# Expert units of 512 rows in a routed two-layer kernel: one early, seven more, then 256 and 128

## The chip, the cores and the metric

The kernel runs on one core of a Trainium2 chip. The metric is the device time of one execution in microseconds (us). Three executions of the kernel before took 748.33, 751.46 and 752.22 us; the median is 751.46 us.

## The reference

Eight batches of eight heads (576 positions, 64 values a head) go through two attentions whose results are added, and the 4608 rows of 512 values then go through one of eight experts each:

```
out_d = softmax(q_d k_d^T / 8) v_d          # q_d, k_d, v_d: means over 4 positions
out_local = softmax(masked q k^T / 8) v     # mask: |i - j| < 4
x = (repeat(out_d, 4) + out_local)          # as 4608 rows of 512
logits = x @ w_gate + modality_bias[modality_id]
e = argmax(logits);  gate = softmax(logits)[e]
out[row] = gate[row] * (relu(x[row] @ w1[e]) @ w2[e])     # w1: 8 x 512 x 1024, w2: 8 x 1024 x 512
```

Computed in numpy on the drawn inputs, the routing sends 1389 rows to expert 1, 2290 to expert 6 and 929 to expert 7, and none to the others. Of the first 2816 rows, 861, 1373 and 582 go there.

## The kernel before

**Attention and routing.** 32 head pairs pass through a software pipeline whose calls are sorted by hand-written phases (PHASE: a step's time in units of one head pair). Row batches are written to a DRAM table `xs`, and each row's number and gate are scattered (L599, one scatter for each 128 rows, from POOL) into `tab`, a DRAM list of rows by expert.

**Units.** An expert works on units of 256 rows that all belong to it. For a unit, POOL reads row numbers from `tab` (`entries`, L804, tile `tg`, one indirect DMA for each 128 rows), gathers the rows from `xs` (`gather`, L814, tile `xg`), and TensorE transposes them (`xsplit`, L836, tile `xt`). Every fp32 operand is split into a rounded fp32r part and a remainder (xh and xl, whi and wlo, hh and hl), and a product is three matmuls. Layer 1 (`compute`, L858) has the weights stationary and the rows moving: 4 chunks of 2 blocks of 4 x 3 matmuls, 96 in all, each of 256 columns. ScalarE and VectorE evict it as hh and hl (L860, L861). Layer 2 (`second`, L905) has 128 rows of the hidden layer stationary and the weights moving: 8 x 3 matmuls of 512 columns for each 128 rows. ScalarE applies the gate (L908), and POOL scatters the rows to the output (L909).

**Weights.** Each unit loads its expert's 4 MB in eight chunks of 512 KB (L763, L766 on the SP queue), each split by ScalarE (L785) and VectorE (L791). Chunks are asked for eight ahead, by `step()`, into a ring of 13.

**Order.** Two early units are taken from the first 2816 rows while the last head pairs run; their rows are gathered before `free`, the point where the attention's loading tiles are given up. Unit 0's rows are split before `free`, unit 1's after it. When the last batch is routed, one table (`late`: lists of full and half units, 25 entries over 16 columns) gives all that remains: 16 units of 256 rows and one of 128. The order is two early units, 15 units, the one of 128, and a last one of 256; a loop at the end takes what is left, and here it takes nothing (37 gathers are 18 x 2 + 1).

```
order = [(True, i, 2) for i in range(KEARLY)] + [(False, i, 2) for i in range(NFULL)]
order.insert(-1, (False, NFULL, 1))
...
            gather(i + 2)
            (moe.compute if H == 2 else moe.compute_half)(Ts[i], Ws[i], Xs[i], step, lambda: split(i + 1))
```

Of the kernel before, what the change touches and what calls it, by code (L numbers as in the profile page):

```python
# [24 lines left out]
NB = 6  # L25
# [9 lines left out]
UNIT = 256  # L35
KEARLY = 2
EB = 5
EARLY = 128 * (9 * (EB // 2) + 4 * (EB % 2))
NFULL = 18 - KEARLY
NLOOP = 8  # L40
# [4 lines left out]
SP0 = ()  # L45
HOLD = 14
NHOLD = 20
GO = 1

# [26 lines left out]
class Consts:  # L76
# [59 lines left out]
    def routing(s, tc, pool, work, psum):  # L136
# [31 lines left out]
        ip = work.tile([128, 2], I32, name="ip")  # L168
        nc.gpsimd.iota(ip, pattern=[[128, 2]], base=0, channel_multiplier=1)
        s.pos = pool.tile([128, 2], F32, name="pos")  # L170
        nc.vector.tensor_copy(s.pos, ip)

    def biases(s, tc, pool, work, rows, psum):
# [4 lines left out]
        mp = psum.tile([128, 36], F32, name="mp", tag="T", bufs=3)  # L178
# [13 lines left out]
class Attention:  # L192
# [61 lines left out]
    def vp(s, n, i):  # L254

        b, hp = divmod(n, 4)
        vw = s.vw[b % 2].rearrange("p (h k) d -> p k h d", k=NB)
        p = s.t["vp", n // 2] = s.ps.tile([96, 2, 4, D], F32, name="vp", tag="T", bufs=3)
# [9 lines left out]
    def tp(s, n, nm):  # L268

        src = s.QK[n // 2]["qk".index(nm)]  # L270
        p = s.t["tp", nm, n] = s.ps.tile([128, 512], F32, name="tp", tag="T", bufs=3)
# [10 lines left out]
    def tpt(s, n, i):  # L282

        p = s.t["tp", "t", n] = s.ps.tile([128, 2, 64], F32, name="tpt", tag="T", bufs=3)
# [42 lines left out]
    def mk(s, n, a):  # L327
        p = s.t["sc", n, a] = s.ps.tile([128, NB, WIN], F32, name="sc", tag="S", bufs=3)
        s.nc.tensor.matmul(p, s.C.identb, s.C.mask, start=True, stop=False, skip_group_check=True)
# [28 lines left out]
    def scd(s, n, i):  # L358

        qd, kd = s.t.pop(("qd", n)), s.t.pop(("kd", n))  # L360
        p = s.t["scd", n] = s.ps.tile([128, 3, 144], F32, name="scd", tag="S", bufs=3)
# [48 lines left out]
    def pdt(s, n, kc):  # L410

        p = s.t["pdt", n, kc] = s.ps.tile([96, 512], F32, name="pdt", tag="T", bufs=3)
# [47 lines left out]
class Router:  # L460
# [6 lines left out]
    def start(s, work):  # L467
# [9 lines left out]
        nc.sync.dma_start(tab.rearrange("(p o x) w -> p o x w", p=128, o=NE),  # L477
                          ft.unsqueeze(1).broadcast_to([128, NE, 36, 2]))
# [20 lines left out]
    def lgt(s, b, i):  # L499
        g0, g1 = ((0, 2), (2, s.t["G", b]))[i]  # L500
        p = s.t["lgt", b, i] = s.ps.tile([128, g1 - g0, 128], F32, name="lgt", tag="T", bufs=3)
# [75 lines left out]
    def xr(s, b, t):  # L577
        if t < s.t["G", b]:
            p = s.t["xr", b, t] = s.ps.tile([128, DM], F32, name="xr", tag="T", bufs=3)
# [36 lines left out]
    def units_of(s, c, add, n, nm):  # L616
# [4 lines left out]
        s.nc.vector.tensor_scalar(ni, ni, 8, None, op0=ALU.logical_shift_right)  # L621
# [4 lines left out]
    def table(s, n, base, U, nm, pool, tag):  # L626
# [4 lines left out]
        m = tp.tile([128, N, N], F32, name=nm + "m")  # L631
# [10 lines left out]
        nc.vector.scalar_tensor_tensor(off, excl, -float(UNIT), base, op0=ALU.mult, op1=ALU.add)  # L642
# [20 lines left out]
        nc.vector.scalar_tensor_tensor(r[:, 0], C.uf[:, :U], float(UNIT), r[:, 0], op0=ALU.mult, op1=ALU.add)  # L663
# [3 lines left out]
    def index(s, r, U, nm, count=None):  # L667

        nc, C, tp = s.nc, s.C, s.tp
        sh = [128, U, 2]  # L670
        idx = tp.tile(sh, I32, name=nm + "idx")
        nc.vector.tensor_tensor(idx, C.pos.unsqueeze(1).broadcast_to(sh), r[:, 0, :U].unsqueeze(2).broadcast_to(sh),
# [10 lines left out]
    def early(s, K):  # L683

        nc, tp = s.nc, s.tp
        n = tp.tile([128, NE], F32, name="en")
        yield from s.units_of((yield from s.counts("e")), 0, n, "e")
        r, _, excl = yield from s.table(n, s.C.ecap, K, "e", None, None)
        s.found = yield from s.index(r, K, "e")
        d = s.d = tp.tile([128, NE], F32, name="dd")  # L690
# [5 lines left out]
        yield  # L696

    def late(s, c, pool):

        nc, tp = s.nc, s.tp  # L700
        n = tp.tile([128, 2 * NE], F32, name="mn")
        base = tp.tile([128, 2 * NE], F32, name="mbase")
        whole(s.units_of(c, UNIT // 2 - 1, n[:, :NE], "m"))
        whole(s.units_of(c, UNIT - 1, n[:, NE:], "mh"))
        nc.vector.tensor_tensor(n[:, NE:], n[:, NE:], n[:, :NE], op=ALU.subtract)
        for i, x in enumerate((s.d, n[:, :NE])):
            nc.vector.scalar_tensor_tensor(base[:, NE * i : NE * i + NE], x, float(UNIT), s.C.ecap, op0=ALU.mult,  # L707
                                           op1=ALU.add)
        nc.vector.tensor_tensor(n[:, :NE], n[:, :NE], s.d, op=ALU.subtract)
# [20 lines left out]
class Moe:  # L730
    def __init__(s, tc, ctx, C, psum, xs, tab, w1, w2, out):
# [7 lines left out]
        s.xb = None  # L739
        s.nw = 13  # L740
# [55 lines left out]
    def entries(s, idx, u, H=2, T=None, h0=0):  # L796

        nc = s.nc
        T = T or s.xa.tile([128, 2, 2], I32, name="tg", bufs=4)
# [19 lines left out]
    def alt(s, key):  # L819

        n = s.turn[key] = s.turn.get(key, -1) + 1
        return s.we if n % 2 else s.xa

    def hidden(s):
        n = s.turn["h"] = s.turn.get("h", -1) + 1
        return [(s.we, s.xb)[n % 2].tile([128, 8, 256], F32R, name=nm) for nm in ("hh", "hl")]

    def xsplit(s, R, H=2):
        nc, C = s.nc, s.C
        pool = s.alt("s")  # L830
        xh = pool.tile([128, 4, 256], F32R, name="xh")
        xl = pool.tile([128, 4, 256], F32R, name="xl")
        for h in range(H):
            p = s.ps.tile([128, 4, 128], F32, name="xt", tag="T", bufs=3)
            for k in range(4):
                nc.tensor.transpose(p[:, k, :], R[:, h, 128 * k : 128 * k + 128], C.ident)  # L836
            yield
# [7 lines left out]
    def compute(s, T, W, X, step=None, mid=None):  # L845
        nc = s.nc
        xh, xl = X
        hh, hl = s.hidden()
        for c in range(4):
# [10 lines left out]
            nc.scalar.activation(hh[:, 2 * c : 2 * c + 2, :], p, AF.Relu)  # L860
            nc.vector.scalar_tensor_tensor(hl[:, 2 * c : 2 * c + 2, :], p, 0.0,  # L861
                                           hh[:, 2 * c : 2 * c + 2, :].bitcast(F32), op0=ALU.max, op1=ALU.subtract)
        if mid:
            mid()
        s.second(T, W, hh, hl, 2, step)

    def compute_half(s, T, W, X, step, mid):
# [4 lines left out]
        for g in range(2):  # L872
            r = s.xp.tile([128, 512], F32, name="o", bufs=3)
            p = s.ps.tile([128, 2, 256], F32, name="l1", tag="S", bufs=3)
# [8 lines left out]
            p = s.ps.tile([128, 4, 128], F32, name="ht", tag="T", bufs=3)  # L883
# [5 lines left out]
        mid()  # L889
        s.second(T, W, hh, hl, 1, step)  # L890

    def second(s, T, W, hh, hl, H, step):

        nc = s.nc
        for h in range(H):
            hs = slice(128 * h, 128 * h + 128)

            first = s.turn["h"] == 0
            p = s.ps.tile([128, DM], F32, name="l2", tag="S" if first else "A", bufs=3 if first else 2)
# [18 lines left out]
def build(tc, q, k, v, mid, w_gate, bias, w1, w2, out):  # L918
    nc = tc.nc
    with ExitStack() as ctx:  # L920
# [5 lines left out]
        tab = dp.tile([NSLOT, 2], I32, name="tab")  # L926
        C = Consts(tc, cp, ps)
        moe = Moe(tc, ctx, C, ps, xs, tab, w1, w2, out)
        with ExitStack() as actx:
# [71 lines left out]
            def rows(u, h):  # L1001
                R[u] = moe.gather(T[u], EARLY, h + 1, R.get(u), h)
                if h:
# [12 lines left out]
            def split(u):  # L1016
                piece(("x", u), lambda: moe.xsplit(E[u][2]), E[u].append)
# [6 lines left out]

            going = {}
# [5 lines left out]
            for i in range(26):  # L1031
# [3 lines left out]
            for i in range(2 * KEARLY):  # L1035
                call(t + 0.5 + 0.6 * i, entries, i // 2, i % 2)
                call(t + 3 + 0.6 * i, rows, i // 2, i % 2)
            for j in range(7):
                call(t + 5.8 + 0.15 * j, split, 0)
# [17 lines left out]
            for j in range(7):  # L1057
                call(free + 1.5 + 0.1 * j, split, 1)
# [23 lines left out]
            early = [E[0] + [W], E[1]]  # L1082

        order = [(True, i, 2) for i in range(KEARLY)] + [(False, i, 2) for i in range(NFULL)]
        order.insert(-1, (False, NFULL, 1))
        Es, Ts, Rs, Xs = {}, {}, {}, {}

        def gather(i):
            if i < len(order):
                ahead, u, H = order[i]  # L1090
                if ahead:
                    Es[i], Ts[i], Rs[i] = early[i][:3]
                else:
                    Es[i], Ts[i] = moe.expert(tei, u), moe.entries(tidx, u, H)
                    Rs[i] = moe.gather(Ts[i], H=H)

        def split(i):
            if i < len(order):
                Xs[i] = early[i][3] if i < KEARLY else whole(moe.xsplit(Rs[i], order[i][2]))

        def step():

            pace.append(0)
            for _ in range(SP0[len(pace) - 1] if len(pace) <= len(SP0) else 1):
                if not todo:
                    return
# [3 lines left out]
        pace = []  # L1110
        Ws = {i: [] for i in range(len(order))}
        Ws[0] = early[0][4]
        todo = [(i, c) for i in range(len(order)) for c in range(8)][len(Ws[0]) :]
        gather(0)
        gather(1)
        split(0)
        for c in range(LEAD - len(Ws[0])):
            i, c = todo.pop(0)
            Ws[i].append(moe.chunk(Es[i], c // 4, c % 4))
        for i, (_, _, H) in enumerate(order):  # L1120
            if i == 0:
                with tc.high_priority():
                    tidx, tei = ro.late(cnt, moe.xp)
            gather(i + 2)
            (moe.compute if H == 2 else moe.compute_half)(Ts[i], Ws[i], Xs[i], step, lambda: split(i + 1))
# [45 lines left out]
```

## Time and profile before

| | |
|---|---|
| median of three runs | 751.46 us |
| the profiled execution: its time | 754.67 us |
| its span, first to last instruction | 753.0 us |
| mean granted TensorE clock | 0.957 |
| TensorE matmuls busy | 705.5 us, 94% of the span |
| VectorE, ScalarE, GpSimd busy | 450.4, 429.3, 293.1 us |
| moved by DMA | 141.55 MB |

Times in the views count from the first instruction of the span. Matmuls are pipelined: the time that one occupies the engine is read from start to start, not from the length printed beside it.

### The profile page before, as it was taken

What the parts mean: (1) busy time and instruction counts of PE and PEld (TensorE: products, weight loads), DVE (VectorE), ACT (ScalarE), POOL (GpSimd) and SP (SyncE); (2) the same over time, 40 slices, a digit from 0 to 9 for tenths busy, and PEclk for the clock granted to TensorE, in tenths of its full rate; (3) what the DMA queues carried; (4) which work ended last, traced back from release to release, by engine and by line L of the source; (5) the groups of instructions that cost most, each with busy time, mean ns of one, the idle gap of its engine ahead of it and who ended that gap; (6) DMA issues with size and microseconds to landing.
All of it is one profiled execution on the core that took longest, in us unless ns stands there. A gap on an engine that the chain in (4) does not pass through costs nothing. (4 is left out here: it accounts for less than half of the span.)

```text
span 753.0 us, 21037 instructions
## 1 busy us (share of the span) xinstructions
PE 705.5 (94%) x8435; PEld 602.7 (80%) x8435; DVE 450.4 (60%) x908; ACT 429.3 (57%) x908; POOL 293.1 (39%) x385
## 2 busy tenths in 40 slices
PE   5999899999969999976999999999999999999995
PEld 3777677776747778875999889998899988999894
DVE  3677476676766695665765555655556556565520
ACT  2667587686756686536665554655545555555520
POOL 7545566637465953035533322322323233121101
PEclk8799899999998999988999999999999999999998
DMA  9899978969874544639997667776677666676500
GB/s 188 170 180 200 145 161 168 170 140 170 150 149 118 110 159 99 188 117 323 304 306 235 212 219 238 226 241 213 210 231 237 239 198 229 200 255 223 167 13 18
DMA packets 201445, 141.55 MB, mean 188 GB/s; under 512 B 133661, under 2 KB 172609, under 8 KB 201346
## 3 DMA queue, kind: packets, MB, share of 16 engines
q1 hardware_dynamic: 193090, 120.96, 62.1%
q0 software_dynamic: 8256, 19.22, 7.4%
q8 instruction: 67, 1.10, 0.7%
q14 instruction: 32, 0.26, 0.1%
HBM read 120.95 MB, written 19.47 MB: 186 GB/s over the span
## 5 line engine op out<-in xcount | busy, mean ns | idle before, releaser
L791 DVE TENSOR_TENSOR wlo<-raw,whi 128x1024 fp32r<-128x1024 f32 x130 | 158.4, 1231 | 134.3 <-ACT whi L785 133.5
L785 ACT CAST whi<-raw 128x1024 fp32r<-128x1024 f32 x130 | 135.0, 1049 | 129.0 <-PE l L858 60.9
L858 PE MATMUL l<-xh,whi 128*128 128x256 f32 x488 | 139.7, 288 | 4.3 <-DVE mn L623 3.7
L858 PE MATMUL l<-xl,whi 128*128 128x256 f32 x488 | 140.7, 289 | 0.0
L858 PE MATMUL l<-xh,wlo 128*128 128x256 f32 x488 | 140.4, 288 | 0.0
L909 POOL DMA_INDIRECT out_dram<-o,tg x37 | 40.0, 1081 | 174.4 <-ACT o L908 134.3
L858 PEld LDWEIGHTS l<-xh,whi 128*128 128x128 f32 x488 | 95.0, 195 | 5.8 <-issue 4.1
L905 PE MATMUL l<-whi,hl 128*128 128x512 f32 x256 | 99.5, 390 | 0.0
L905 PE MATMUL l<-wlo,hh 128*128 128x512 f32 x256 | 99.4, 391 | 0.0
L905 PE MATMUL l<-whi,hh 128*128 128x512 f32 x256 | 97.6, 395 | 0.0
L858 PEld LDWEIGHTS l<-xl,whi 128*128 128x128 f32 x488 | 94.9, 194 | 0.8
L858 PEld LDWEIGHTS l<-xh,wlo 128*128 128x128 f32 x488 | 95.0, 195 | 0.2 <-issue 0.2
L861 DVE SCALAR_TENSOR_TENSOR hl<-l,hh 128x512 fp32r<-128x512 f32 x72 | 49.4, 686 | 28.9 <-ACT hh L860 28.9
L804 POOL DMA_INDIRECT tg<-tab,midx x33 | 37.8, 1145 | 72.8 <-DMA out_dram<-o,tg 66.7
L860 ACT ACTIVATE hh<-l 128x512 fp32r<-128x512 f32 x72 | 42.7, 593 | 35.7 <-PE l L858 35.7
L392 POOL TENSOR_TENSOR le<-le,zr 128x384 f32<-128x384 f32 x32 | 26.7, 834 | 91.5 <-DVE zr L388 72.9
L814 POOL DMA_INDIRECT xg<-xs,tg x37 | 40.8, 1102 | 53.0 <-DMA tg<-tab,midx 35.2
L599 POOL DMA_INDIRECT tab<-ig,si x36 | 38.2, 1060 | 54.1 <-DVE mbase L707 33.7
L905 PEld LDWEIGHTS l<-wlo,hh 128*128 128x128 f32 x256 | 48.0, 188 | 10.2
L408 ACT COPY Pw<-lt 32x288 f32<-32x288 f32 x128 | 54.9, 429 | 2.2
L905 PEld LDWEIGHTS l<-whi,hh 128*128 128x128 f32 x256 | 48.1, 188 | 9.9 <-issue 0.5
L905 PEld LDWEIGHTS l<-whi,hl 128*128 128x128 f32 x256 | 48.1, 188 | 9.6
(216 smaller groups left out, 1373.5 us busy)
## 6 DMA issues: line engine op xcount, KB each, us to landing
raw<-in_moe_w_dram SPq DMA_DIRECT2D x152, 512.0 KB
vw<-in_v_dram SPq DMA_DIRECT2D x53, 192.0 KB
xs<-R SPq DMA_DIRECT2D x36, 256.0 KB
qt<-in_q_dram SPq DMA_DIRECT2D x30, 288.0 KB
kt<-in_k_dram SPq DMA_DIRECT2D x30, 288.0 KB
vw<-in_v_dram SPq DMA_DIRECT2D x15, 96.0 KB
xg<-xs,tg POOLq DMA_INDIRECT x37, 5.2
out_dram<-o,tg POOLq DMA_INDIRECT x37, 3.5
```

What stands on the lines that cost most here:

```text
L392: s.nc.gpsimd.tensor_tensor(e, e, z[:, : 2 * NB].unsqueeze(2).broadcast_to([128, 2 * NB, WIN]), op=ALU.mult)
L408: s.nc.scalar.copy(s.Pw[n % NPW][r, :, j, :SUB], s.t["lt", n][r, :, :SUB])
L599: i = nc.gpsimd.indirect_dma_start(out=s.tab[:, :], out_offset=bass.IndirectOffsetOnAxis(ap=C.si[:, t : t + 1], axis=0), in_=C.ig[:, t, :] ...
L785: nc.scalar.copy(hi, raw)
L791: nc.vector.tensor_tensor(lo, raw, hi.bitcast(F32), op=ALU.subtract)
L804: nc.gpsimd.indirect_dma_start(out=T[:, h, :], out_offset=None, in_=s.tab[:, :], in_offset=bass.IndirectOffsetOnAxis(ap=idx[:, u, h : h + ...
L814: s.gathered = nc.gpsimd.indirect_dma_start(out=R[:, h, :], out_offset=None, in_=s.xs[:n, :], in_offset=bass.IndirectOffsetOnAxis(ap=T[:, ...
L858: nc.tensor.matmul(p[:, f, :], a[:, k, fs], x[:, k, :], start=(k == 0 and i == 0), stop=(k == 3 and i == 2))
L860: nc.scalar.activation(hh[:, 2 * c : 2 * c + 2, :], p, AF.Relu)
L861: nc.vector.scalar_tensor_tensor(hl[:, 2 * c : 2 * c + 2, :], p, 0.0, hh[:, 2 * c : 2 * c + 2, :].bitcast(F32), op0=ALU.max, op1=ALU.subtract)
L905: nc.tensor.matmul(p, a[:, f, hs], x[:, f % 2, :], start=(f == 0 and i == 0), stop=(f == 7 and i == 2))
L909: nc.gpsimd.indirect_dma_start(out=s.out[:, :], out_offset=bass.IndirectOffsetOnAxis(ap=T[:, h, 0:1], axis=0), in_=o, in_offset=None, boun ...
```

## The change

The unit becomes 512 rows. One early unit (KEARLY = 1) is taken from the first 2816 rows, seven more ("pairs", NPAIR) come from a small table of their own (7 entries over 8 columns), made first; a second table (`late`, 21 entries over 16 columns) gives two units of 256, one of 128, and up to 18 for the loop. On the drawn counts the pairs are one of expert 1, four of expert 6 and two of expert 7; then one unit of 256 each of experts 1 and 6 and the one of 128 of expert 1 are left, and nothing for the loop.

Layer 1 of a 512 unit has 96 matmuls of 512 columns; layer 2 goes over four blocks of 128 rows. hh and hl have one buffer instead of two, xh and xl too. The next unit's rows are split in three places of layer 2 (two blocks, one, one) instead of one. The early unit's split stands wholly after `free`. The weight ring has 12 chunks. Table entries past the end point behind `tab`, which is 4608 rows longer, and gathers pass over rows out of bounds; the early unit's tile of rows is therefore cleared first, on POOL.

```diff
-UNIT = 256
-KEARLY = 2
+KEARLY = 1
-NFULL = 18 - KEARLY
-NLOOP = 8
+NPAIR = 8 - KEARLY
+NFULL = 2
+NLOOP = 18
-HOLD = 14
-NHOLD = 20
+HOLD = 9
+NHOLD = 16
+SPLIT = {4: (2, 1, 1), 2: (2,), 1: (2,)}
...
+    def pairs(s, c, pool):
+        nc, tp = s.nc, s.tp
+        n = tp.tile([128, NE], F32, name="pn")
+        base = tp.tile([128, NE], F32, name="pbase")
+        whole(s.units_of(c, 127, n, "p", 9))
+        nc.vector.tensor_tensor(n, n, s.d, op=ALU.subtract)
+        nc.vector.scalar_tensor_tensor(base, s.d, 512.0, s.C.ecap, op0=ALU.mult, op1=ALU.add)
+        r, _, s.pexcl = whole(s.table(n, base, NPAIR, "p", pool, "o", 512))
+        s.pn = n
+        return whole(s.index(r, NPAIR, "p", H=4))
...
-        s.nw = 13
+        s.nw = 12
...
-        R = R or s.xa.tile([128, 2, DM], F32, name="xg", bufs=2)
+        R = R or s.unit_rows()
...
-                in_offset=bass.IndirectOffsetOnAxis(ap=T[:, h, 0:1], axis=0))
+                in_offset=bass.IndirectOffsetOnAxis(ap=T[:, h, 0:1], axis=0), bounds_check=n - 1, oob_is_err=False)
...
     def hidden(s):
-        n = s.turn["h"] = s.turn.get("h", -1) + 1
-        return [(s.we, s.xb)[n % 2].tile([128, 8, 256], F32R, name=nm) for nm in ("hh", "hl")]
+        s.turn["h"] = s.turn.get("h", -1) + 1
+        return [s.xb.tile([128, 8, 512], F32R, name=nm) for nm in ("hh", "hl")]
...
+        N = 128 * H
         for c in range(4):
...
-            p = s.ps.tile([128, 2, 256], F32, name="l1", tag="S", bufs=3)
             for f in range(2):
+                if H == 4 or f == 0:
+                    p = s.ps.tile([128, 4 // H, N], F32, name="l1", tag="S", bufs=SB)
                 fs = slice(128 * f, 128 * f + 128)
                 for k in range(4):
                     for i, (a, x) in enumerate(((wh, xh), (wh, xl), (wl, xh))):
-                        nc.tensor.matmul(p[:, f, :], a[:, k, fs], x[:, k, :], start=(k == 0 and i == 0),
+                        nc.tensor.matmul(p[:, 0 if H == 4 else f, :], a[:, k, fs], x[:, k, :N], start=(k == 0 and i == 0),
                                          stop=(k == 3 and i == 2))
...
+            def clear(u):
+                R[u] = moe.unit_rows()
+                nc.gpsimd.memset(R[u], 0.0)
+            for u in range(KEARLY):
+                call(4.3 + u, clear, u)
...
-            for j in range(7):
-                call(t + 5.8 + 0.15 * j, split, 0)
...
-            for j in range(7):
-                call(free + 1.5 + 0.1 * j, split, 1)
+            for j in range(13):
+                call(free + 0.4 + 0.15 * j, split, 0)
...
+        order = [("e", i, 4) for i in range(KEARLY)] + [("p", i, 4) for i in range(NPAIR)]
+        order += [("m", i, 2) for i in range(NFULL)]
+        order.insert(-1, ("m", NFULL, 1))
...
-        gather(0)
-        gather(1)
-        split(0)
...
             if i == 0:
                 with tc.high_priority():
-                    tidx, tei = ro.late(cnt, moe.xp)
+                    lists["p"] = ro.pairs(cnt, moe.xp)
+                gather(1)
+            if i == 1:
+                lists["m"] = ro.late(cnt, moe.xp)
             gather(i + 2)
```

## Rows read from the trace of the kernel before

**Rows 1.** The page: TensorE's busy share, and its granted clock in 40 slices.
```profile
PE 705.5 (94%) x8435; PEld 602.7 (80%) x8435; DVE 450.4 (60%) x908; ACT 429.3 (57%) x908; POOL 293.1 (39%) x385
...
PEclk8799899999998999988999999999999999999998
```

**Rows 2.** Windows: start:end, length, each engine's busy us, clock, DMA share, GB/s.
```profile
321.00:332.00 11.00, 7.33 (x36) 6.83 (x34) 9.26 (x32) 4.63 (x7) 5.53 (x5) 0.69 0.29 105
332.00:355.00 23.00, 17.23 (x97) 14.50 (x95) 11.31 (x19) 10.14 (x13) 10.34 (x11) 0.91 0.80 256
...
381.05:684.14 303.09, 303.09 (x1977) 278.23 (x1976) 174.02 (x184) 162.80 (x210) 85.28 (x77) 1.00 0.69 228
```

**Rows 3.** TensorE in order of time, one settled unit: start, length, instruction, idle before.
```profile
381.05 0.28 PE L858 MATMUL l<-xh,whl 128*128 128x256 f32 x1
...
392.56 1.04 PE L836 MATMUL xt<-ident,xg 128*128 128x128 f32 x8
393.36 0.48 PE L905 MATMUL l<-whi,hh 128*128 128x512 f32 x1
...
404.36 0.28 PE L858 MATMUL l<-xh,whi 128*128 128x256 f32 x1
```

**Rows 4.** TensorE in order of time, from the early units on.
```profile
282.49 0.50 PE L858 MATMUL l<-xh,whi 128*128 128x256 f32 x2
...
298.04 0.60 PE L836 MATMUL xt<-ident,xg 128*128 128x128 f32 x4
...
308.02 1.28 PE L490 MATMUL lg<-X,wg 128*32 128x320 f32 x16
...
324.89 0.55 PE L858 MATMUL l<-xh,whi 128*128 128x256 f32 x1 [3.67 <-DVE mn L623]
...
345.70 0.39 PE L905 MATMUL l<-whi,hl 128*128 128x512 f32 x1
...
346.61 0.39 PE L905 MATMUL l<-wlo,hh 128*128 128x512 f32 x1
351.19 1.11 PE L836 MATMUL xt<-ident,xg 128*128 128x128 f32 x4 [4.19 <-DMA xg<-xs,tg]
353.38 1.12 PE L836 MATMUL xt<-ident,xg 128*128 128x128 f32 x4 [1.08 <-DMA xg<-xs,tg]
355.17 1.01 PE L858 MATMUL l<-xh,whi 128*128 128x256 f32 x3 [0.67 <-ACT xh L839]
...
684.14 0.28 PE L858 MATMUL l<-xh,whl 128*128 128x256 f32 x1
```

**Rows 5.** POOL in order of time, where the routing ends.
```profile
331.23 0.96 POOL L599 DMA_INDIRECT tab<-ig,si  x1 [0.30 <-issue]
...
338.27 0.99 POOL L909 DMA_INDIRECT out_dram<-o,tg  x1 [4.61 <-issue]
339.57 0.98 POOL L804 DMA_INDIRECT tg<-tab,midx  x1 [0.30 <-DMA raw<-in_moe_w_dram]
...
346.48 0.95 POOL L814 DMA_INDIRECT xg<-xs,tg  x1 [4.66 <-DMA tg<-tab,midx]
```

**Rows 6.** VectorE in order of time, the table of the remaining units.
```profile
321.46 0.16 DVE L612 COPY mc<-cp 128x8 f32<-128x8 f32 x1
...
327.53 0.17 DVE L638 TENSOR_TENSOR mexcl<-mincl,mn 128x16 f32<-128x16 f32 x1
327.62 0.57 DVE L651 TENSOR_TENSOR o<-mincl,uf 128x400 f32<-128x400 f32 x1
...
333.42 0.23 DVE L676 CAST mei<-mr 128x17 int32<-128x17 f32 x1
```

**Rows 7.** The page's costliest groups: the evictions of layer 1.
```profile
L861 DVE SCALAR_TENSOR_TENSOR hl<-l,hh 128x512 fp32r<-128x512 f32 x72 | 49.4, 686 | 28.9 <-ACT hh L860 28.9
...
L860 ACT ACTIVATE hh<-l 128x512 fp32r<-128x512 f32 x72 | 42.7, 593 | 35.7 <-PE l L858 35.7
```

**Rows 8.** POOL in order of time: three memsets.
```profile
5.76 3.11 POOL L218 MEMSET Pw<- 128x1152 f32 x3
```

More of the change, by code (lines that the diff above doesn't have):

```diff
@@ L614, in counts, with units_of @@
         return c
[L616 removed]
+    def units_of(s, c, add, n, nm, bits=8):
         ni = s.tp.tile([128, NE], I32, name=nm + "ni")
@@ L624, in units_of, with table @@
         yield
-    def table(s, n, base, U, nm, pool, tag):
+    def table(s, n, base, U, nm, pool, tag, unit=256):
         nc, C, tp = s.nc, s.C, s.tp
         N = n.shape[1]
-        m = tp.tile([128, N, N], F32, name=nm + "m")
+        m = (pool.tile([128, DM], F32, name=tag, bufs=3)[:, : N * N].rearrange("p (a b) -> p a b", a=N) if tag else
+             tp.tile([128, N, N], F32, name=nm + "m"))
         incl = tp.tile([128, N], F32, name=nm + "incl")
@@ L641, in table @@
         off = tp.tile([128, N], F32, name=nm + "off")
-        nc.vector.scalar_tensor_tensor(off, excl, -float(UNIT), base, op0=ALU.mult, op1=ALU.add)
+        nc.vector.scalar_tensor_tensor(off, excl, -float(unit), base, op0=ALU.mult, op1=ALU.add)
         yield
@@ L681, in index, with taken @@
         return idx, ei
[L683 to L690, printed above, removed]
+    def taken(s, n, excl, K, nm):
+        nc = s.nc
+        d = s.tp.tile([128, NE], F32, name=nm + "d")
         nc.vector.tensor_scalar(d, excl, -1.0, float(K), op0=ALU.mult, op1=ALU.add)
@@ L925, in build @@
         xs = dp.tile([NTOK + 1, DM], F32, name="xs")
-        tab = dp.tile([NSLOT, 2], I32, name="tab")
+        tab = dp.tile([NSLOT + CAP, 2], I32, name="tab")
         C = Consts(tc, cp, ps)
@@ L1030, in build @@
             t = 4 * (EB - 1) + max(P[x] for x in P if x[:2] == "st") + 0.02
-            for i in range(26):
+            for i in range(29):
                 call(min(t, 4 * (EB - 1) + P["ch2"] + 0.1) + 0.07 * i, first)
@@ L1034, in build @@
                 call(t + 1 + 0.1 * u, expert, u)
-            for i in range(2 * KEARLY):
-                call(t + 0.5 + 0.6 * i, entries, i // 2, i % 2)
-                call(t + 3 + 0.6 * i, rows, i // 2, i % 2)
-            for j in range(7):
-                call(t + 5.8 + 0.15 * j, split, 0)
+            for i in range(4 * KEARLY):
+                call(t + 0.5 + 0.6 * i, entries, i // 4, i % 4)
+                call(t + 3 + 0.6 * i, rows, i // 4, i % 4)
             for c in range(2):
@@ L1081, in build @@
                 ro.store(b, i)
[L1082 to L1086, printed above, removed]
+            early = [E[0] + [W]]
+        order = [("e", i, 4) for i in range(KEARLY)] + [("p", i, 4) for i in range(NPAIR)]
+        order += [("m", i, 2) for i in range(NFULL)]
+        order.insert(-1, ("m", NFULL, 1))
+        lists, Es, Ts, Rs, Xs, parts = {}, {}, {}, {}, {}, {}
@@ L1088, in gather @@
         def gather(i):
             if i < len(order):
[L1090 to L1097, printed above, removed]
-            if i < len(order):
-                Xs[i] = early[i][3] if i < KEARLY else whole(moe.xsplit(Rs[i], order[i][2]))
+                nm, u, H = order[i]
@@ new lines, in gather, with split @@
+                idx, ei = lists[nm]
+                Es[i], Ts[i] = moe.expert(ei, u), moe.entries(idx, u, H)
+                Rs[i] = moe.gather(Ts[i], H=H)
+        def split(i, h):
+            if i < len(order):
+                if not h:
+                    parts[i] = moe.xsplit(Rs[i], order[i][2])
+                n = len(SPLIT[order[i - 1][2]]) - 1
+                for _ in range(SPLIT[order[i - 1][2]][min(h, n)] if h <= n else 0):
+                    for x in (next(parts[i], None) for _ in range(3)):
+                        Xs[i] = x or Xs.get(i)
+                if h == order[i - 1][2] - 1:
+                    next(parts[i], None)
@@ L1101, in step @@
         def step():
[L1103 to L1106, printed above, removed]
+            if todo:
                 i, c = todo.pop(0)
                 Ws[i].append(moe.chunk(Es[i], c // 4, c % 4))
-        pace = []
         Ws = {i: [] for i in range(len(order))}
-        Ws[0] = early[0][4]
+        Es[0], Ts[0], Rs[0], Xs[0], Ws[0] = early[0]
         todo = [(i, c) for i in range(len(order)) for c in range(8)][len(Ws[0]) :]
-        gather(0)
```

123 lines of the change are left out of this document (69 added, 54 removed).

## The prediction

> **What bounds the kernel now.** The page comes first: TensorE is busy 94% of the span at a clock near full speed, and no other engine passes 60% [rows 1]. The page's chain of what ended last holds only the last few us, so I cut the span into windows. From 381.05 to 684.14 TensorE is busy every one of 303.09 us at clock 1.00, while VectorE and ScalarE are busy 174.02 and 162.80 us and DMA 0.69 [rows 2]. There the bound is TensorE's own stream, and neither fewer weight loads nor fewer splits can shorten it.
>
> In that stream I read starts [rows 3]. Layer 1 runs from 381.05 to 392.56: 11.51 us for 96 matmuls of 256 columns, 0.120 us each. Eight transposes take 0.80. Layer 2 runs from 393.36 to 404.36: 11.00 us for 48 matmuls of 512 columns, 0.229 each. Twice the columns cost 1.91 times as much, so a part of each matmul's time does not grow with its columns. A unit takes 23.31 us, and thirteen of them fill the 303.09.
>
> Ahead of it is the head, 282.49 to 355.17, where the two early units mix with the attention's end [rows 4]. TensorE waits there: 3.67 us before 324.89, 4.19 before 351.19, then 1.08 and 0.67, in all 9.6. Of these, 5.3 are waits for gathered rows. The clock is 0.69 in 321 to 332 and 0.91 in 332 to 355 [rows 2]; the first full unit after 355.17 takes 25.88 us, up to 381.05, 2.57 above the settled 23.31.
>
> So the span is 355.17 + 25.88 + 13 x 23.31 + 68.86, where 68.86 is what follows 684.14: a unit of 256, the one of 128, the last of 256, and the end. I call the start of the first unit after the early rows S; here it is 355.17.
>
> **The change part by part.** From S on, 14 units of 256 become seven of 512, and the last three units and the end stay.
>
> *Layer 1, wider.* Two units had 192 matmuls of 0.120: 23.02 us. One unit of 512 has 96 of 512 columns. Layer 2 already issues matmuls of that width, in fp32r, at 0.229 on average [rows 3]; undisturbed, four of them take 0.91 us from 345.70 to 346.61, 0.2275 each [rows 4]. That gives 21.8 to 22.0, a saving of 1.0 to 1.2 a unit; I take 1.1, since width and type are layer 2's. Layer 2 (96 matmuls) and the transposes (16) are as before. A unit is 45.5 us against 46.63, and seven save 7.7 (7.1 to 8.3).
>
> The Trainium skill (TensorE: Matmul & The Clock Gate, Back-to-back issue gap) gives a single matmul's warm gap as columns over 2.4 GHz plus 2.5 ns. By it 192 narrow ones would take 20.96 us and 96 wide ones 20.72, so that an estimate from that page saves 0.24 a unit and 1.7 in seven. The rows show a larger part that does not grow (0.120 and 0.229), so the sum stays with the rows.
>
> *Weights.* Eleven sets of eight chunks instead of nineteen. All of it lies beside TensorE's stream, where DMA, ScalarE and VectorE have room [rows 2]: no gain, no cost. With 12 ring places a chunk replaces one read a unit and a half earlier, long done.
>
> *One buffer for hh, hl and for xh, xl.* hh is overwritten after the next unit's first layer-1 block, which TensorE issues after the old unit's layer 2, the last reader; 12 wide matmuls, 2.7 us, lie between. The eviction of a block, 0.593 and then 0.686 us [rows 7], fits in those 2.7. xh's last reader is the layer 1 just before its next split. I cost both at nothing; if a wait appeared it would be at most one eviction, 1.3 us at each of ten boundaries, 13 in all.
>
> *Early part.* The cleared tile is 128 x 2048; three memsets of 1152 took 3.11 [rows 8], so 1.8 us of POOL once, in a stretch where POOL has slack: 0 to 1.8, taken as 0. The 512 longer entries of the fill and the bounds check ride on DMAs that are there already.
>
> *The head.* TensorE's work in 282.49 to 355.17 was 72.68 less 9.6 of waits, less some 3.3 of slow clock (the missing clock of the two windows is 11 x 0.31 + 23 x 0.09 = 5.5 us, a part of it in the waits), so 59.8; the two units are 45.0 of it and the rest 14.8. Now unit 0 costs 192 x 0.229 = 44.0, and the rest 14.8 + 1.2 for two blocks whose transposes stood before 282. But unit 0 cannot begin at 282.49. All its four blocks must be split, and the last split stands about where unit 1's second block stood, at 298.04 [rows 4]. What TensorE did for unit 0 up to there, about 9 us, has nothing to fill its place. Without that work in front of them the attention's last steps come sooner, perhaps by 5 us. Idle 2 to 9, taken as 6.
>
> Then the next rows. Before, the logits of the last batch at 308.02 led to row numbers at 333.42, and 12 us of this are the table on VectorE [rows 4, 6]: seven operations of 400 elements at 0.57. The pairs' table has 56 elements for these, near the 0.17 of the 16-element row: 3 to 5 us earlier. But the row numbers must wait for the last scatter into `tab` at 331.23, and then they stood behind an output scatter at 338.27 [rows 5]. From the first read at 339.57 to S was 15.6 us; four blocks instead of two add two reads, two gathers (1.3 each, as from 338.27 to 339.57) and two splits, 4 to 6. Against this stand the earlier table and the earlier logits, 5 to 10. So the rows come between 345 and 356, and TensorE ends unit 0 at 282.49 + 44.0 + 16.0 + 6 = 348.5. I take 2 us of waiting: S = 350.5, 4.7 earlier than before; bounds 344 (no idle, no wait) and 363 (waits and clock loss as before on top). Of the slow first unit's 2.57 I keep half, since a shorter wait costs less clock.
>
> *Sum.* -7.7 - 4.7 - 1.3 = -13.7. The profiled span 753.0 becomes 739.3. Its own time, 754.67, is 3.2 over the median of the runs and its span 1.5 over it, so I take the difference from the median: 751.46 - 13.7 = 737.8.
>
> **The rivals.** *The fixed part does not shrink in layer 1.* If a 512-column matmul with the rows moving took 0.240, nothing is saved: 737.8 + 7.7 = 745.5. For it: no row shows that operand order at that width. Against: layer 2's are alike in width and type. The same page's gap would put the time at 743.8. Chance 0.12.
>
> *The next rows come late (the other side).* POOL runs its queue in order. If the eight reads and gathers of unit 1 stand behind the output scatters of unit 0's blocks, they wait for layer 2. Behind the last of four, the first read goes out at about 350 and S is 350 + 15.6 + 5 = 370: 19.5 later, with all of the clock's 2.57, 758.6. Each block earlier is 24 matmuls, 5.5 us less: 753 and 747. For it: the read at 339.57 did stand behind an output scatter that had waited 4.61 [rows 5]. Against: the table and the reads come early in the program's order, and that scatter was unit 0's, whose layer 2 now comes later. Slower than 755.2 needs S beyond 367. Chance 0.20, a third of it slower, two fifths within 0.5%.
>
> *The single buffer waits.* Ten boundaries at 1.3 us give back 13: 750.8. For it: hidden layers alternated between two tiles. Against: the order of TensorE's own queue, above. Chance 0.06.
>
> *The change doesn't do what it says.* If no expert had 512 early rows, or the loop had to run, a unit of 44 us would be empty or units would be added; the counts 861, 1389, 2290 and 929 exclude it.
>
> **How the numbers follow.** The forecast with S between 344 and 356 has 0.62 and its own range is 729 to 744. A measurement here can tell some 0.5%, 3.8 us. Faster by more: 0.62 + 0.11 of the first rival + 0.06 of the second + 0.03 of the third = 0.82. Within it, 747.7 to 755.2: 0.08 + 0.03 = 0.11. Slower: 0.07. The range from 728 (bounds of the saving and of S, no clock loss) to 751 takes in the first rival and the mild end of the second, and leaves out about 0.17.
>
> **What would show it.** Right: layer 1 of a pair starts its matmuls 0.227 to 0.229 apart, pairs follow every 45.5 us without a wait at either boundary, TensorE is busy all of seven pairs at clock 1.00, S lies near 350, and 69 us follow the last pair. Wrong: a pitch of 0.24 in layer 1; a wait on hh or xh at each boundary; POOL's reads for unit 1 behind an output scatter and TensorE idle for over 10 us before S; or unit 0's first matmul later than 300, which would move S by as much.

## The result and the profile after

| device time, us | before | after |
|---|---|---|
| median of 20 runs | 748.71 | 739.29 |
| lowest and highest | 742.38, 754.34 | 734.93, 746.46 |
| profiled execution, its span | 754.67, 753.0 | 734.93, 733.1 |
| mean granted clock in it | 0.957 | 0.977 |

The medians differ by 9.4 us. The ratio, taken over the runs of each kernel that lie within 1.5% of its fastest, is 0.988 with a 95% interval of [0.985, 0.991]: 1.2% off. The forecast was 737.8 us and 13.7 off. The two profiled executions overstate the change, for that of before is slower than all its 20 timed runs and that of after is the fastest of its own. Their spans differ by 19.9 us, and the first work below is to take that number apart.

The page of after, its first part and the clock in 40 slices, answers to [rows 1].

```profile
PE 689.5 (94%) x7667; PEld 551.1 (75%) x7667; DVE 381.7 (52%) x874; ACT 369.9 (50%) x844; POOL 290.3 (40%) x386
...
PEclk9799999999989999999999999999999999999998
```

TensorE has 768 matmuls fewer and is as large a share of the span as it was. DMA moved 107.92 MB in place of 141.55.

TensorE of after in order of time (start, length, instruction, idle before), for [rows 3] and [rows 4].

```profile
268.98 0.95 PE L369 MATMUL scd<-kd,qd 64*64 64x144 f32 x12
...
281.56 0.65 PE L864 MATMUL xt<-ident,xg 128*128 128x128 f32 x4 [0.21 <-ACT PdT L425]
283.86 0.98 PE L889 MATMUL l<-xh,whi 128*128 128x512 f32 x3 [1.01 <-ACT xh L867]
...
290.52 1.28 PE L494 MATMUL lg<-X,wg 128*32 128x320 f32 x16
...
312.05 0.39 PE L937 MATMUL l<-whi,hh 128*128 128x512 f32 x1
...
324.11 0.40 PE L937 MATMUL l<-whi,hl 128*128 128x512 f32 x1
327.80 1.11 PE L864 MATMUL xt<-ident,xg 128*128 128x128 f32 x4 [3.29 <-DMA xg<-xs,tg]
...
340.89 0.40 PE L889 MATMUL l<-xh,whi 128*128 128x512 f32 x1
...
389.11 0.39 PE L889 MATMUL l<-xh,whi 128*128 128x512 f32 x1
...
484.05 0.39 PE L889 MATMUL l<-xh,whi 128*128 128x512 f32 x1
484.29 0.40 PE L889 MATMUL l<-xl,whi 128*128 128x512 f32 x1
484.52 0.39 PE L889 MATMUL l<-xh,wlo 128*128 128x512 f32 x1
484.75 0.40 PE L889 MATMUL l<-xh,whi 128*128 128x512 f32 x1
...
573.52 0.39 PE L889 MATMUL l<-xh,whi 128*128 128x512 f32 x1
573.75 0.39 PE L889 MATMUL l<-xl,whi 128*128 128x512 f32 x1
573.98 0.39 PE L889 MATMUL l<-xh,wlo 128*128 128x512 f32 x1
574.21 0.40 PE L889 MATMUL l<-xh,whi 128*128 128x512 f32 x1
```

The `scd` row at 268.98 is the last head pair's deep score, the same work as in before, where it starts at 279.33:

```profile
279.33 0.95 PE L365 MATMUL scd<-kd,qd 64*64 64x144 f32 x12
```

340.89 is S, the first matmul of the first pair. Layer 1 has 512 columns from the early unit at 283.86 on. The time from one start to the next, called the pitch from here on, is 0.233 near 484 and 0.230 near 573: it is not one number, and this became the main question.

The windows of after (start:end, length, busy us of each engine, clock, DMA share, GB/s) answer to [rows 2].

```profile
321.00:332.00 11.00, 7.71 (x33) 6.07 (x32) 6.89 (x7) 7.09 (x9) 8.01 (x7) 0.84 0.94 316
400.00:660.00 260.00, 260.00 (x1177) 212.38 (x1176) 95.74 (x110) 95.06 (x132) 55.45 (x54) 1.00 0.38 127
```

From 400 to 660 TensorE has no gap, across five boundaries of pairs. The waits of TensorE from 300 to 370 are two:

```profile
PE xt L864 <- DMA xg<-xs,tg: 3.3, 1, 3.3
PE l L889 <- DVE hl L894: 1.0, 1, 1.0
```

POOL in order of time answers to [rows 5]: the last scatter into `tab`, then the four reads (first and last), the four gathers (first and last), and the first output scatter.

```profile
309.57 0.96 POOL L603 DMA_INDIRECT tab<-ig,si  x1 [0.30 <-issue]
314.65 0.97 POOL L833 DMA_INDIRECT tg<-tab,pidx  x1 [4.12 <-issue]
...
318.45 1.48 POOL L833 DMA_INDIRECT tg<-tab,pidx  x1 [0.31 <-issue]
321.93 1.07 POOL L843 DMA_INDIRECT xg<-xs,tg  x1 [1.99 <-DMA raw<-in_moe_w_dram]
...
326.37 1.61 POOL L843 DMA_INDIRECT xg<-xs,tg  x1 [0.30 <-issue]
...
334.06 1.02 POOL L941 DMA_INDIRECT out_dram<-o,tg  x1 [0.30 <-issue]
```

VectorE, the pairs' table, for [rows 6]:

```profile
302.91 0.17 DVE L616 COPY mc<-cp 128x8 f32<-128x8 f32 x1 [2.31 <-PE cp L613]
...
305.53 0.21 DVE L656 TENSOR_TENSOR o<-pincl,uf 128x56 f32<-128x56 f32 x1
...
308.50 0.17 DVE L683 TENSOR_TENSOR pidx<-pos,pr 128x28 int32<-128x28 f32 x1
```

The table takes 5.6 us where it took 12.0, with operations of 0.21 in place of 0.57. It is done at 308.67, before the last scatter starts at 309.57, so the reads don't wait for it. They start 4.12 us after that scatter's instruction has ended; the profile names no reason. A wait for the scatter's landing fits, for issues on `tab` around it land 4.3 to 7.6 us later, but it is not shown. They stand ahead of every output scatter.

**Cutting the spans in three.** The last deep score (D) and S divide an execution into the attention, the head and the units. Repeats of both kernels show how much of each part is spread.

| profiled execution | 0 to D | clock there | D to S | S to end |
|---|---|---|---|---|
| before | 279.3 | 0.93 | 75.8 | 397.8 |
| before, again | 280.0 | 0.93 | 77.4 | 397.6 |
| after | 269.0 | 0.96 | 71.9 | 392.2 |
| after, again | 277.5 | 0.94 | 73.9 | 391.6 |
| after, third | 271.2 | 0.96 | 76.1 | 393.6 |
| after, fourth | 275.5 | 0.94 | 73.8 | 391.5 |

Ten of the 19.9 us are attention, which goes with the granted clock: length times clock is 258 to 261 in all six rows. In seven profiles of padded forms of after (below) D lies between 272.6 and 284.0, so nothing shows that the change shortens the attention. The head is 76.6 on the mean before and 73.9 after, 2.7 less; the units are 397.7 and 392.2, 5.5 less. That makes 8.2 of the 9.4; the other 1.2 lies within the attention's spread and is not resolved. The head's 2.7 is not sharp either: 71.9 to 76.1 after and 75.8 to 77.4 before overlap. The five padded kernels with wide layers, in six profiles, have 72.7 to 75.6, and a third profile with the units of before has 76.5, so that some 2 us are likely and no more is shown.

### The profile page after: what moved, and what is told of

Same layout as the page of the kernel before. It is cut to its first block, busy times and chain, and to the rows that moved or that the text cites. A ratio compares the mean times of both kernels' runs of the same rounds, so it can differ in the third digit from the quotient of the medians.

```text
span 733.1 us, 19052 instructions
## 1 busy us (share of the span) xinstructions
PE 689.5 (94%) x7667; PEld 551.1 (75%) x7667; DVE 381.7 (52%) x874; ACT 369.9 (50%) x844; POOL 290.3 (40%) x386
## 2 busy tenths in 40 slices
DMA packets 175965, 107.92 MB, mean 147 GB/s; under 512 B 132765, under 2 KB 155329, under 8 KB 175874
## 5 line engine op out<-in xcount | busy, mean ns | idle before, releaser
L820 DVE TENSOR_TENSOR wlo<-raw,whi 128x1024 fp32r<-128x1024 f32 x74 | 92.0, 1246 | 125.8 <-ACT whi L814 125.0
L814 ACT CAST whi<-raw 128x1024 fp32r<-128x1024 f32 x74 | 77.6, 1050 | 71.3 <-PE l L889 48.0
L937 PE MATMUL l<-whi,hh 128*128 128x512 f32 x256 | 101.6, 401 | 0.0
L889 PE MATMUL l<-xh,whi 128*128 128x512 f32 (+1 forms) x256 | 95.4, 375 | 1.0 <-ACT xh L867 1.0
L889 PE MATMUL l<-xl,whi 128*128 128x512 f32 (+1 forms) x256 | 95.2, 372 | 0.0
L889 PE MATMUL l<-xh,wlo 128*128 128x512 f32 (+1 forms) x256 | 95.2, 372 | 0.0
L940 ACT ACTIVATE o<-l,tg 128x512 f32<-128x512 f32 x37 | 25.5, 688 | 95.9 <-PE l L937 62.7
L937 PEld LDWEIGHTS l<-whi,hh 128*128 128x128 f32 x256 | 48.3, 189 | 10.7
L889 PEld LDWEIGHTS l<-xh,whi 128*128 128x128 f32 x256 | 48.0, 188 | 10.0 <-ACT xh L867 1.3
L889 PEld LDWEIGHTS l<-xh,wlo 128*128 128x128 f32 x256 | 48.1, 188 | 9.3 <-issue 0.5
L889 PEld LDWEIGHTS l<-xl,whi 128*128 128x128 f32 x256 | 48.1, 188 | 8.6
```

Of the source, the lines that this page charges most:

```text
L814: nc.scalar.copy(hi, raw)
L820: nc.vector.tensor_tensor(lo, raw, hi.bitcast(F32), op=ALU.subtract)
L889: nc.tensor.matmul(p[:, 0 if H == 4 else f, :], a[:, k, fs], x[:, k, :N], start=(k == 0 and i == 0), stop=(k == 3 and i == 2))
L937: nc.tensor.matmul(p, a[:, f, hs], x[:, f % 2, :], start=(f == 0 and i == 0), stop=(f == 7 and i == 2))
L940: nc.scalar.mul(o, p, T[:, h, 1:2].bitcast(F32))
```

## The experiments

Ratios are to runs of the kernel before that were made together with the experiment's, with 95% intervals; an experiment of a single run has none, and the narrow one has none on record.

**Repeats of both kernels.** No edit. Three more sets of runs of after and a single run of before.

> The changed kernel once more, as the base of this call. The theory says that most of the 19.9 us between the two profiled spans that exceeds the 9.4 us between the medians is the attention's own run-to-run spread (the last deep score matmul starts at 279.3 us before and 269.0 after, in a part that the change hardly touches): this trace should show that start anywhere from 268 to 280, and the stretch from there to the first pair (71.9 us in the first trace) and from there to the end the same within 3 us. If the change itself made the attention shorter, the start is near 269 again. In the pairs the wide matmuls start 0.227 or 0.234 apart, by weight tile, as in the first trace.

> The kernel before once more, for a second trace. Theory of the two terms: in the first traces the stretch from the last deep score matmuls to the first unit after the early rows (S) is 75.9 us before against 71.9 to 75.1 in four runs of the 512 kernel and its shifted forms, and the stretch from S to the end is 397.8 against 391.6 to 393. A second trace should give the second stretch again within 1.5 us, and the first within some 4, so that the head's term is small and the pairs' term the larger. If the head's gain is as large as it looked in the first two traces (14.3 us in S itself), S here is near 355 and its attention ends near 279 again.

> The changed kernel beside it, as the base of this call: 6 to 11 us over it, if the shift by 32 gives its 5.5 us and the later transposes theirs; the stretch from S to the end 391 to 393 as in its other traces.

> The changed kernel beside it: S to the end 391.6 to 393.6 us again.

After measured 746.58 (0.988 [0.983, 0.993]), 748.76 (0.988 [0.982, 0.994]) and 744.35 (0.992 [0.989, 0.996]); before, in a single run, 756.85. The parts are in the table above. The spacings of the settled pairs repeat to 0.01 us in all four profiles of after: 46.26, 45.88, 46.41, 45.86, 45.91, mean 46.06. The forecast was 45.5. So the shortfall is a property of the program and not of a run.

**Where the tiles start.** In after, layers 1 and 2 both have a pitch of 0.228 or of 0.233, by weight tile. The change made the table of unit numbers shorter (21 entries for 25), which moved the tiles laid out behind it by 32 bytes. By the addresses of the compiled program (no profile shows them), the weight places 6 to 11 and hh and hl start at 448 modulo 512, the places 0 to 5 and xh and xl at 480. In before, the weights and the hidden tiles all start at 480, and the rows' xh and xl, which alternate between two places, at 480 and 96. The test pads a tile that comes early in the pool by 8, 24 or 40 entries, which are 32, 96 or 160 bytes (the first is shown):

```diff
-        zr = work.tile([128, DM // 128], F32, name="zr")
+        zr = work.tile([128, DM // 128 + 8], F32, name="zr")[:, : DM // 128]
```

> The same instructions in the same order; only the tiles behind one small work tile lie 32 bytes further, so that weights, rows and hidden layers all start at 32 modulo 64. Theory of the address: the mixed pitch (0.227 where stationary and moving tile agree modulo 64, 0.234 where they don't) becomes 0.227 throughout, a pair takes 45.4 us instead of 46.1 to 46.2, and eight units of 512 give back 5 to 6.5 us against the changed kernel. Rival, traffic of the other engines or the granted clock: the mix stays and the time is the same within 1 us.

> The same instructions again, with those tiles 96 bytes further than in the changed kernel: all start at 32 modulo 64, but the two groups differ modulo 128 (32 and 96). If agreement modulo 64 decides, this equals the shift by 32, 5 to 6.5 us under the changed kernel. If it takes agreement modulo 128 or more, the mixed pitch stays and the time is that of the changed kernel within 1 us.

> The same instructions as the changed kernel, the tiles 160 bytes further: they agree with the others modulo 128 and differ modulo 512. If agreement modulo 128 is enough, 0.2275 throughout and a settled pair of 45.4 us as with the shift by 32; if 256 or 512 is needed, 0.233 in the same places as with the shift by 96 and 46.0 a pair.

> The kernel shifted by 32 bytes once more, beside the changed kernel, for the time alone. Theory of the address: S to the end 386 us against 391.6 to 393.6, and a time 5 to 6.5 us under the changed kernel's, of which the runs' spread (some 10 us from the lowest to the highest of either) may hide a half.

Mean start-to-start times of the 512-column matmuls between 400 and 640 us, where the two operands start alike modulo 512 and where they do not, in ns (each matmul sorted by its two addresses, gaps at a change of instruction left out):

| kernel | layer 1 alike | layer 1 not | layer 2 alike | layer 2 not |
|---|---|---|---|---|
| after, again: 32 bytes apart | 227.7 | 233.2 | 228.5 | 233.3 |
| + 32 bytes: all at 480 | 227.4 | none | 227.2 | none |
| + 96 bytes: 64 apart | 227.8 | 233.3 | 228.0 | 233.3 |
| + 160 bytes: 128 apart | 227.6 | 232.8 | 228.4 | 232.7 |

So neither likeness modulo 64 nor modulo 128 is enough; a distance of 256 bytes was not tried. The instruction lists of all of these are identical on every engine. TensorE with 32 bytes more, the start of three pairs and a stretch of layer 2:

```profile
404.21 0.39 PE L889 MATMUL l<-xh,whi 128*128 128x512 f32 x1
...
450.19 0.39 PE L889 MATMUL l<-xh,whi 128*128 128x512 f32 x1
...
488.33 0.39 PE L937 MATMUL l<-whi,hl 128*128 128x512 f32 x1
488.55 0.39 PE L937 MATMUL l<-wlo,hh 128*128 128x512 f32 x1
488.78 0.39 PE L937 MATMUL l<-whi,hh 128*128 128x512 f32 x1
489.01 0.39 PE L937 MATMUL l<-whi,hl 128*128 128x512 f32 x1
489.23 0.39 PE L937 MATMUL l<-wlo,hh 128*128 128x512 f32 x1
```

Five pair spacings are now 45.98, 45.39, 45.30, 45.54, 45.42, mean 45.53, and in the second profile of the same kernel the same within 0.01. S to end is 386.0 and 388.1. The whole time is 746.71 (0.985 [0.979, 0.992]) and 741.84 (0.988 [0.984, 0.992]) with 32 bytes, 751.76 (0.994 [0.990, 0.997]) with 96, and 743.67 in a single run with 160. Both times the ratio of the kernel with 32 bytes is lower than that of after by 0.003 to 0.004, with intervals that overlap: the pitch and the spacings are shown, a gain in the time of the run is not.

**The same question put to before.** The iota of expert numbers is dropped and its values are copied from the longer one, which moves before's tiles by 32 bytes:

```diff
-        ie = work.tile([128, NE], I32, name="ie")
-        nc.gpsimd.iota(ie, pattern=[[1, NE]], base=0, channel_multiplier=0)
+        iu = work.tile([128, NUMAX], I32, name="iu")
+        nc.gpsimd.iota(iu, pattern=[[1, NUMAX]], base=0, channel_multiplier=0)
...
-        nc.vector.tensor_copy(s.ef, ie)
+        nc.vector.tensor_copy(s.ef, iu[:, :NE])
```

> The kernel before with one work tile of 32 bytes less, so that the tiles behind it start at 0 modulo 64 instead of 32, against 32 for the others: the misplacement that the change brought, put into the kernel before. Theory of the address: layer 2 starts its matmuls 0.2275 apart where hh and the weights agree and 0.233 where not, half of them, 0.15 us a unit; for the 256-column matmuls of layer 1 no trace shows the price yet, between 0 and the same 6 ns each (7 of 13 ring places, 0.3 us a unit). A settled unit takes 23.45 to 23.8 us instead of 23.31. Rival, that the slow pitch belongs to the 512 units: 23.31 as before.

Half a miss. Layer 2 shows the two pitches, 228.5 and 233.1 to 233.3, where before has 227.4 throughout. But layer 1 with its 256 columns became faster with the weight tiles that moved to 448: 116.7 beside rows at 480 and 118.4 beside rows at 96. With the weights that stayed at 480 it is 119.9 beside either, as in before. The two nearly cancel: a unit is 23.36 on the mean in place of 23.31 (754.61 in a single run). The kernel before had, by its sizes alone, the placement that is best for its layer 2.

**Narrow layer 1.** On the kernel with 32 bytes more, layer 1 of a 512 unit goes back to 256 columns, 192 matmuls, all else as it is:

```diff
-                for k in range(4):
-                    for i, (a, x) in enumerate(((wh, xh), (wh, xl), (wl, xh))):
-                        nc.tensor.matmul(p[:, 0 if H == 4 else f, :], a[:, k, fs], x[:, k, :N], start=(k == 0 and i == 0),
-                                         stop=(k == 3 and i == 2))
+                for w in range(0, N, 256):
+                    for k, i in ((k, i) for k in range(4) for i in range(3)):
+                        nc.tensor.matmul(p[:, 0 if H == 4 else f, w : w + 256], (wh, wh, wl)[i][:, k, fs],
+                                         (xh, xl, xh)[i][:, k, w : w + 256], start=(k == 0 and i == 0), stop=(k == 3 and i == 2))
```

> The shift by 32 bytes, and layer 1 of the 512 units issued as before in matmuls of 256 columns, 192 instead of 96 a unit, all else as it is. Theory of the fixed part: 192 at 0.120 against 96 at 0.2275 is 1.2 us more in each of eight units, 9.6 us over the kernel shifted by 32. Rival, a fixed part of 2.5 ns: 0.24 a unit, 2 us over it.

The median was 758.23, but the six runs lie between 745.96 and 762.38, too far apart to tell the 9.6 us of the theory from the rival's 2. The profile tells. Its windows, the first pair and the second:

```profile
345.74:399.70 53.96, 50.73 (x306) 44.58 (x304) 25.36 (x47) 19.30 (x27) 24.95 (x22) 0.97 0.47 150
399.70:446.40 46.70, 46.70 (x306) 42.70 (x305) 17.32 (x21) 17.46 (x24) 13.27 (x13) 1.00 0.41 136
```

A settled pair is 46.69, that is 1.16 more than 45.53: the width is worth what the sum said, 1.1 a pair. It is also what two units of before take, 46.63, with twice the weight loads and splits. By the Trainium skill (TensorE: Matmul & The Clock Gate, Back-to-back issue gap) the warm gap of a single matmul has a fixed part of 2.5 ns, and the estimate from it was 0.24 a pair; these runs do not bear it out. From D to the end the kernel takes 473.9 where the four profiles with 32 bytes more and wide layers take 460.3 to 463.7: 12.2 more on the mean, where the theory has 9.6 and the rival 2. Before takes 473.7 and 475.1: without the width the larger units show no gain here, though some of the 12.2 are the gaps below.

S to end is 402.7, some 16 above its base, and 7 of that lie in the first pair, 53.96 against 46.0 to 47.7, where the width accounts for 1.2. In part it is only S that comes early: D to S is 71.2, the shortest of all, and from D to the second pair the kernel takes 125.1 against 121.6 on the mean of those four, 3.6 more, of which two units' width is 2.3. TensorE's waits in that pair and three of its matmuls:

```profile
PE l L889 <- issue: 3.1, 9, 0.4
```

```profile
350.94 0.28 PE L889 MATMUL l<-xh,wlo 128*128 128x256 f32 x1
351.49 0.36 PE L889 MATMUL l<-xh,whi 128*128 128x256 f32 x1 [0.27 <-issue]
352.22 0.37 PE L889 MATMUL l<-xl,whi 128*128 128x256 f32 x1 [0.36 <-issue]
```

Single matmuls come late for nothing that the profile shows, and the clock is 0.97. Why is open, and it is one profile. The first unit of before issues matmuls of the same width while DMA is twice as busy, and has no such gap in its window:

```profile
355.17:381.05 25.88, 25.88 (x152) 23.96 (x153) 19.33 (x20) 16.57 (x20) 13.09 (x11) 0.89 0.93 307
```

**The next rows' split later.** The rows of the first pair make TensorE wait 3.3 to 4.7 us some 60 us behind D in the four profiles of after. Both kernels here have the 32 bytes more. The theory: with the split further back in the early unit's layer 2, that layer covers the wait. The rival: the rows' landing sets S and the wait only moves. The second kernel has (0, 0, 0, 4) in place of (0, 0, 2, 2).

```diff
-                n = len(SPLIT[order[i - 1][2]]) - 1
-                for _ in range(SPLIT[order[i - 1][2]][min(h, n)] if h <= n else 0):
+                at = (0, 0, 2, 2) if i == 1 else SPLIT[order[i - 1][2]]; n = len(at) - 1
+                for _ in range(at[min(h, n)] if h <= n else 0):
```

> The shift by 32 bytes, and during the early unit's layer 2 the next unit's transposes stand before its third and fourth block of rows (two each) instead of the first three. In the changed kernel the first of them waited 3.3 us for gathered rows on TensorE's queue, and the matmuls behind it ran for 2.3 us at the lower clock. Theory that this wait is what is left of the head's loss: S comes 3 to 4.5 us earlier against the last deep score matmuls than the 72 to 75 of the other runs, about 70, and the time is 3 to 4 us under the kernel shifted by 32. Rival, the weights or the splits are late next: S stays within 1.5 us and the wait turns up before layer 1 of the first pair.

> As the last one, but the next unit's transposes during the early unit's layer 2 stand behind 72 of its 96 matmuls (three blocks) and behind 94 (the fourth); in the last one the first of them still stood behind 52, where it stands in the changed kernel, and waited 4.7 us for rows. Theory that TensorE's queue is what loses the time: the rows have landed when the transposes come up, the wait and the slow clock behind it go, and the stretch from the last deep score matmuls to S falls from 72 to 75 us to 68 to 71; against it stands at most 1.3 us for the fourth block's eviction just before layer 1. The time falls 2 to 5 us under the kernel shifted by 32. Rival, the rows themselves are the bound: the wait moves to the new place and S stays.

The first (741.29, 0.983 [0.977, 0.989]) told little: the schedule put the first transposes behind as many of layer 2's matmuls as in after, and they waited 4.73. In the second (747.74, 0.987 [0.981, 0.993]) three blocks come behind 72 and the fourth behind 94 of layer 2's 96 matmuls. TensorE's waits from 310 to 358, and its rows just ahead of S at 354.97:

```profile
PE xt L864 <- DMA xg<-xs,tg: 3.2, 3, 1.6
PE xt L864 <- DVE wlo L820: 1.8, 1, 1.8
```

```profile
351.02 0.60 PE L864 MATMUL xt<-ident,xg 128*128 128x128 f32 x4
...
352.19 0.63 PE L864 MATMUL xt<-ident,xg 128*128 128x128 f32 x4
354.59 0.63 PE L864 MATMUL xt<-ident,xg 128*128 128x128 f32 x4 [1.77 <-DVE wlo L820]
354.97 0.72 PE L889 MATMUL l<-xh,whi 128*128 128x512 f32 x2
```

The rows are still waited for, three times, 3.2 us in all. The fourth block's transposes are at 351.02. Those at 352.19 and 354.59 read the second pair's rows (by the program's order): here the schedule put them ahead of S, behind which they stand in the other kernels, and the wait of 1.8 is theirs. So this kernel has 2 us ahead of S that the question didn't ask for. D to S is 74.8 and 75.2, where after has 71.9 to 76.1 and the kernel with 32 bytes more 74.3 and 75.6. A gain of the expected 3 us and more does not show, and the rival is not refuted; with the second pair's transposes in the way it isn't proven either. The first transposes of these rows start about 61 us behind D in every kernel with 512 units (58.2 to 62.9; before, 71.9 to 72.9).

## Why the prediction was right, and where its sizes were off

**The bound.** Right. TensorE is busy all of 400 to 660 at clock 1.00, and fewer loads and splits (32 MB, 128 operations) gave nothing that a stretch shows: a settled pair of the narrow kernel takes 46.69, two units of before with twice the loads 46.63.

**Layer 1, wider: the mis-sized term.** "A unit is 45.5 us against 46.63, and seven save 7.7." The mechanism held: 227.4 ns for a 512-column matmul where the tiles start alike, and 45.53 a pair in that kernel, 46.69 with the narrow form. The change itself has 46.06, because it also moved half of the weight tiles and the hidden layer against their partners, at 5 to 6 ns for each matmul so placed. Nothing in the working looked at where a tile starts. Of 7.7 and 1.3, the change got 5.5 from S on: 2.8 in the five settled spacings (233.14 for ten units before), 0.9 in the first pair (48.05 on the mean of four against 48.96 for the first two units in the two profiles of before), and 1.8 in the rest. With the tiles moved back by 32 bytes S to end is 386.0 to 388.1 in the four profiles so placed and otherwise wide, about 11 less than before: 7.7 for seven pairs, 1.3 in the first pair beyond its share, and some 2 us that the sum did not have. Of these 2, 0.8 are eight transposes that stand ahead of S now (116 of them follow S, 124 before); the rest no run explains.

**The slow first unit.** "I keep half" of 2.57, a gain of 1.3, on the reason that a shorter wait costs less clock. The clock came back whole: the first pair has 1.00 in all four profiles of after, where the first unit of before has 0.89 and 0.91. But that pair is still 2.0 us longer than a settled one, so that 0.3 were gained and not 1.3. In two of the four it waits 1.0 and 1.8 for VectorE's eviction; for the other two nothing is named.

**The head.** Taken as 4.7 earlier, measured 2.7, with the spread said above. The waits came out as forecast on the whole, 8 us: TensorE is idle for 7.3 to 9.1 us between D and S, 8.0 on the mean, where it was 9.2 and 10.7. The parts are others: 3.3 to 4.5 around the start of unit 0 and not 6, and 3.3 to 4.7 for rows and not 2. The mis-sized term is the clock: the sum for S adds 44.0 and 16.0 us of work and none of the 3.3 of slow clock that it took off before, but from D to S the granted clock is 0.98, 0.98, 0.91 and 0.95 (0.93 and 0.92 before). The time in which TensorE works is 64.6 to 68.8, on the mean 65.9, against 66.6: 0.7 less where the sum has 3.

One placement was wrong too: "the last split stands about where unit 1's second block stood, at 298.04". That is 18.7 us behind D in before; in after the last split is 12.6 behind D, and the first matmul of unit 0 14.9 behind D, where it was 3.2. That is better than the step said. As the prediction had it, the attention's tail came sooner: the last logits are 21.5 behind D in place of 28.7, 7 us where 5 were guessed, and the table saves 6.4 where 3 to 5 were. The rows are transposed 12 us sooner (60 behind D in the four profiles of after, 72 before), but TensorE then still has some 43 of the 96 matmuls of the early unit's layer 2, about 10 us, and four blocks to transpose ahead of S, so that little of the 12 reaches it. Whether another order within layer 2 would change this, the two experiments with the split leave open.

**One buffer.** Right: no wait on hh, hl, xh or xl at any settled boundary. The wait on `hl` shown above, 1.0, is inside the first pair (at 361.49): a layer-1 matmul, which does not read hl, waits for VectorE's eviction of a block. It is part of that pair's 48.22 and is gone in the pairs behind it. So it is not the rival's wait, which would come back at each boundary.

**The rivals.** The fixed part that does not shrink: refuted by the pitch and by the narrow form. Late reads on POOL: refuted, the first output scatter stands at 334.06 behind all four gathers. The single buffer: refuted. The change not doing what it says: 37 gathers, and layer 1 in units of 512.

**The number.** 737.8 against 739.29 is closer than the working deserves, and in part luck. The forecast was made from the median of three runs, 751.46, and that of twenty is 2.8 lower; the saving was 4.3 smaller than forecast. The two errors have opposite signs. From 748.71 the same working gives 735.0, which is 4.3 off.

## What to carry to other kernels

Cut the spans of two kernels at one and the same instruction and repeat both before reading a difference of two profiles: here ten of twenty us went with the clock in a part that the change hardly touches. A wider moving operand pays where TensorE's stream is the bound, by the part of a matmul's time that does not grow with its columns, read from two widths in the same trace. When a change alters the size of any tile, compare the pitch by weight tile afterwards, since tiles that only moved can take back part of the gain; here they took half of a pair's.

## What the runs showed of the hardware

- The start-to-start time of fp32r matmuls of 512 columns goes by where the stationary and the moving tile start in a partition: 227 to 229 ns when they are alike modulo 512 bytes, 233.2 when they are 32 bytes apart, 233.3 at 64, 232.7 to 232.8 at 128. With 256 columns the effect has the other sign: 119.9 when alike modulo 512 and at 128 apart, 116.7 at 32 apart and 118.4 at 160 (one profile). The mechanism is open, and 256 bytes apart was not tried.
- Settled stretches repeat to 0.01 us for each pair between executions, while the attention of the same program varies from 269.0 to 277.5 us with its granted clock, 0.94 to 0.96.
- In one profile, 256-column matmuls of the first pair show gaps of 0.2 to 0.45 us before single matmuls that no wait explains. Width and DMA traffic alone don't bring them: the first unit of before, of the same width, shows none with DMA 0.93 busy. With 512 columns two profiles of ten have single gaps without a named cause in the first pair, of 0.7 in one and up to 0.9 in the other, and eight have none. The cause is open.
